# Mask rows of two batches copied by SyncE's transfers instead of VectorE, in a fused block-sparse attention and MLP kernel

## The chip, the cores and the metric

The kernel runs on one core of a Trainium2 chip. A core has five engines with queues of their own, each working in order: TensorE (PE, matmuls, with weight loads shown apart as PEld), VectorE (DVE), ScalarE (ACT), GpSimd (POOL), and SyncE (SP), which here does nothing but issue DMA transfers. They share an on-chip memory of 128 partitions (SBUF) and an accumulator memory for matmul results (PSUM); the inputs and outputs lie in the chip's main memory and move by DMA. The metric is the time of one execution in device microseconds.

## The reference

```python
# batch, n_heads, seq, head_dim = 4, 8, 768, 64
k_rep = k.reshape(B, H, 12, 64, D).mean(axis=3)            # one mean key per block of 64
gate = einsum('bhsd,bhnd->bhsn', q, k_rep)                 # causal blocks only, else -1e9
top_idx = argsort(gate, axis=-1)[..., -3:]                 # the 3 best blocks of each query
mask = blocks in top_idx or the query's own block, and key position <= query position
attn = softmax(where(mask, 0.125 * q @ k.T, -1e9))
x = (attn @ v), heads side by side: 3072 tokens x 512
h = x @ w_in                                               # 512 x 2048
g = 0.5 * h * (1 + tanh(sqrt(2 / pi) * (h + 0.044715 * h**3)))
out = g @ w_out                                            # 2048 x 512
```

Inputs and output are float32; the kernel computes its matmuls in float16, except for the gate.

## The kernel before

The work is cut by batch and, in it, by pair of heads: pairs 0 to 15, four to a batch (`p`, with `HP = 4`). Every pair goes through `pre(p)`, then `heads2(p)` (batch 0) or `heads(p)` (batches 1 to 3). When the four pairs of a batch are done, `s1(b)` computes the first layer of the MLP and its GELU, and the second layer follows: `s2_plain` for batch 0, and `s2` for the others, where the product is done with seven half-size products instead of eight (sums on DVE: `w_sums` for the weights, `sums` for the activations). The last batch does a part of the first layer in that way too (`s1_seven`).

In `pre(p)` for a pair of batches 1 to 3, four transfers of SyncE bring each of keys and queries in a layout that one DVE transpose (L564) turns into 128 rows (two heads of 64 dimensions) by 768 positions, in float32. From the keys DVE takes the block sums (L621); two copies with a cast to float16, one per head (`kc_all`, drawn by the helper `copy`, whose lines are L363 for ACT, L365 for POOL and L367 for DVE), bring them to `kT16[i][h]`, rows 0 to 63. The queries go the same way into `qT16[i][h]`. PE multiplies queries and block sums (the gate, L687), DVE transposes the result (L703), finds the third largest of 12 for each query with ten `max` instructions (L719), and writes a small table `madd` of 0 and -1 (L724).

The mask reaches the scores as 12 more rows: rows 64 to 75 of `qT16[i][h]` hold the mask of a query for 12 blocks, and the same rows of `kT16[i][h]` hold a constant pattern (`fill`, L520), so that a score matmul of 76 rows (L1046) adds the mask by itself. For these rows `madd` has to be transposed. For batch 1 (`byPE`) PE does it (L756) into a PSUM bank. For batches 2 and 3 a transposing DMA of SyncE (`mask_dma`, L763) writes a tile `mT`, of which there are two. Then `mc(h)` copies the 12 rows of one head and 640 positions into `qT16[i][h]`, two copies per pair; from `mT` DVE does them. The score matmuls of a head wait for the cast key, the cast query and this copy.

In `heads(p)` the scores of a unit go to a wide PSUM tile (L1046), ACT takes the exponential (L1059), POOL clears what lies above the diagonal (L1073), and PE multiplies by the values (L1085). DVE normalizes (L968, L969). The first layer is L1122, its GELU L1134; the second layer of batch 0 is L1322, the seven products are L1372 with their joins on DVE at L1421. Loads are L394 and L400, output rows L1347 and L1456, transposing DMAs of the normalized output L993. The weights are loaded by POOL's queue (L460); a small transfer on SyncE (L1567) waits for w_in to have landed, and the loads of batch 1 stand behind it.

The order is fixed in the file. Each step is an `Op` with its possible engines and a planning cost for each. `ORDER` lists the numbers of the steps in the order in which they are emitted, `BUFFER` says which buffer each takes, and `ENGINE` which steps run on another engine than their first; each engine executes its own steps in the order of that list. The list may also hold dummy matmuls (`warm`, L1524) which multiply zeros into a free bank; 72 are defined, and those that the list names are run. Here 39 are.

Of the kernel before, what the change touches and what calls it, by code (L numbers as in the profile page):

```python
# [189 lines left out]
    "POOL": [  # L190
        586, 587, 646, 647, 707, 972, 973, 1035, 1036, 1097, 1098,
        1159, 1160, 1425, 1489, 1551, 1612]}


class Op:
# [40 lines left out]
def kernel(  # L236
# [9 lines left out]
    nc = tc.nc  # L246
# [111 lines left out]
    add = plan.add  # L358
# [1268 lines left out]
```

## Time and profile before

| | us |
|---|---|
| median of 3 runs | 257.65 |
| lowest, highest | 257.62, 258.15 |
| the profiled execution | 257.76 |
| span in its profile, first to last instruction | 256.04 |
| granted TensorE clock | 1.0 of full |

| engine | busy, us | share | instructions |
|---|---|---|---|
| PE | 246.5 | 96% | 2485 |
| DVE | 191.4 | 75% | 539 |
| ACT | 176.4 | 69% | 225 |
| POOL | 84.3 | 33% | 163 |

A row of the profile names the line, the engine, the operation, `out<-in` by the program's names, sizes and a count; `L1046 PE ... wide<-qT,kT` writes a wide PSUM tile from `qT` and `kT`. In the groups, busy time in all and the mean in ns of one follow, then the idle time of the engine just ahead of these instructions and what ended it. In rows in order of time the first two numbers are start and length in us; in square brackets stands how long the engine was idle before and what released it. A tile's view gives minimum, median and maximum in ns. In a table of stages, each engine's busy time stands with its instruction count. The chain of waits is the chain of work that ended last, followed back from the last instruction. A busy PE is not PE at its peak: matmuls are pipelined, so the distance of starts, not the length of one, says how much PE time a matmul takes.

### The profile page before, as it was taken

The numbers are of one execution on the slowest core, as the hardware profiler recorded it, in microseconds if no ns is written. First come the engines' busy times: TensorE is split into PE (matmuls) and PEld (weight loads), VectorE is DVE, ScalarE is ACT, GpSimd is POOL, SyncE is SP. The second block draws the span as 40 slices with busy tenths as digits, with TensorE's granted clock in tenths as the row PEclk, the third lists the DMA queues.
The fourth block names the chain that finished last, engine by engine and source line by source line (L and its number), as shares of the span: only waits on it lengthen the run. The fifth ranks groups of instructions, "written<-read, shape, count | busy, mean of one in ns | idle before, by whom it ended". The sixth has DMA issues, their size and how long they took to land.

```text
span 256.0 us, 6451 instructions
## 1 busy us (share of the span) xinstructions
PE 246.5 (96%) x2485; PEld 171.2 (67%) x2485; DVE 191.4 (75%) x539; ACT 176.4 (69%) x225; POOL 84.3 (33%) x163
## 2 busy tenths in 40 slices
PE   7889999999998999999899999999999999999994
PEld 5667686555554566555578888555777786766883
DVE  2769751041989889989999999699889665579954
ACT  2399997634898998667969884566889957557300
POOL 8465970000239366223053853100056620000000
PEclk9999999999999999999999999999999999999999
DMA  8997599999989995999899699532112520040024
GB/s 164 218 208 166 94 212 191 213 161 157 184 142 165 153 143 99 172 179 199 127 174 110 144 188 166 118 94 69 26 34 72 64 74 1 3 165 0 3 82 164
DMA packets 130927, 32.62 MB, mean 127 GB/s; under 512 B 124528, under 2 KB 126928, under 8 KB 130896
## 3 DMA queue, kind: packets, MB, share of 16 engines
q1 hardware_dynamic: 126160, 27.62, 65.4%
q0 software_dynamic: 3136, 4.19, 9.7%
q10 hardware_dynamic: 1600, 0.39, 0.8%
q8 instruction: 19, 0.31, 0.5%
q14 instruction: 12, 0.10, 0.1%
HBM read 27.26 MB, written 6.29 MB: 131 GB/s over the span
## 4 chain that ended last, share of the span: by engine, by line
PE 51%; DVE 16%; SPq 11%; DMA 10%; POOL 4%; issue 3%; ACT 3%; ACTq 1%; DVEq 0%; POOLq 0%
PE bank L1372 17%; PE wide L1122 10%; SPq L400 9%; PE wide L1046 6%; PE wide L1211 5%; DMA w_in<-in_moe_w_in_dram 5%; PE bank L1085 5%; PE bank L1322 3%; DVE qT L367 3%; DMA sd<-in_k_dram 3%; DVE sel L719 2%; DVE s L564 2%; DVE XS L1309 2%; DMA G<-in_q_dram 2%; ACT ats L882 1%
## 5 line engine op out<-in xcount | busy, mean ns | idle before, releaser
L1122 PE MATMUL wide<-xT,w_in 128*128 128x384 f16 x416 | 72.6, 326 | 0.0
L1059 ACT ACTIVATE ats<-wide 128x896 f16<-128x896 f32 x72 | 63.4, 915 | 8.9 <-PE wide L1046 6.2
L1134 ACT ACTIVATE G<-wide 128x768 f16<-128x768 f32 x52 | 42.1, 810 | 27.3 <-PE wide L1122 27.0
L1122 PEld LDWEIGHTS <-w_in 128*128 128x128 f16 x416 | 40.0, 98 | 26.8 <-issue 1.3
L1073 POOL TENSOR_SCALAR_AFFINE_SELECT ats<-ats 128x256 f16<-128x256 f16 x72 | 33.3, 475 | 60.3 <-ACT ats L1059 60.2
L1046 PE MATMUL wide<-qT,kT 76*128 76x512 f16 (+3 forms) x192 | 39.1, 305 | 0.1
L564 DVE STREAM_TRANSPOSE s<-sd 128x768 f32<-128x768 f32 x24 | 23.1, 968 | 18.7 <-DMA sd<-in_k_dram 17.2
L1372 PE MATMUL bank<-w_out,G 128*128 128x256 f16 x216 | 31.4, 272 | 0.0
L1372 PEld LDWEIGHTS <-G 128*128 128x128 f16 x288 | 26.9, 98 | 6.0 <-issue 0.3
L1322 PE MATMUL bank<-w_out,G 128*128 128x512 f16 x96 | 28.1, 379 | 0.0
L365 POOL CAST kT<-s 64x768 f16<-64x768 f32 x17 | 15.2, 891 | 37.5 <-DVE s L564 37.0
L1421 DVE TENSOR_TENSOR osb<-bank,osb 128x512 f32<-128x512 f32 (+1 forms) x38 | 22.1, 592 | 5.1 <-PE bank L1372 4.5
L1085 PEld LDWEIGHTS <-ats 128*128 128x128 f16 x504 | 22.2, 98 | 3.9 <-POOL ats L1073 0.4
L1085 PE MATMUL bank<-v,ats 128*128 128x65 f16 x504 | 24.4, 194 | 0.2 <-POOL ats L1073 0.2
L1046 PEld LDWEIGHTS <-kT 76*128 76x128 f16 x192 | 17.3, 98 | 10.5 <-issue 0.8
L1372 PEld LDWEIGHTS <-XS 128*128 128x128 f16 x216 | 20.0, 98 | 5.5 <-DVE XS L1309 1.5
L1372 PE MATMUL bank<-TS,XS 128*128 128x256 f16 x144 | 22.0, 272 | 0.8 <-DVE XS L1309 0.7
L882 ACT ACTIVATE ats<-wide 128x1024 f16<-128x1024 f32 (+3 forms) x24 | 20.8, 924 | 1.3 <-PE wide L863 0.8
L365 POOL CAST v<-vsd 128x768 f16<-128x768 f32 x13 | 11.4, 875 | 13.8 <-DMA vsd<-in_v_dram 8.8
L969 DVE TENSOR_TENSOR xn<-bank,zr 128x384 f16<-128x384 f32 x24 | 13.4, 558 | 0.8
L719 DVE MAX8 sel<-sel 128x8 f32<-128x12 f32 x160 | 13.2, 158 | 0.6
L1322 PEld LDWEIGHTS <-G 128*128 128x128 f16 x96 | 8.9, 98 | 6.1 <-issue 0.3
(120 smaller groups left out, 358.6 us busy)
## 6 DMA issues: line engine op xcount, KB each, us to landing
out_dram<-osb SPq DMA_DIRECT2D x23, 256.0 KB
vsd<-in_v_dram SPq DMA_DIRECT2D x26, 192.0 KB
sd<-in_k_dram SPq DMA_DIRECT2D x48, 96.0 KB
sd<-in_q_dram SPq DMA_DIRECT2D x48, 96.0 KB
w_in<-in_moe_w_in_dram POOLq DMA_DIRECT2D x2, 1024.0 KB, 11.5
w_out<-in_moe_w_out_dram POOLq DMA_DIRECT2D x2, 1024.0 KB, 14.5
G<-in_k_dram SPq DMA_DIRECT2D x4, 192.0 KB
G<-in_q_dram SPq DMA_DIRECT2D x4, 192.0 KB
```

The lines of the kernel that those rows point to most:

```text
L365: nc.gpsimd.tensor_copy(out=out, in_=in_)
L400: nc.sync.dma_start(out=T[key, p][64 * hh + 32 * a:64 * hh + 32 * a + 32], in_=SRC[key][b, 2 * hp + hh].rearrange("(t i) (a j) -> a i t j" ...
L564: nc.vector.transpose(out=T[key + "T32", p], in_=T[key, p].rearrange("p t j -> p (t j)"))
L882: nc.scalar.activation(out=T["at", u][:, :, 0:n], in_=plan.buf[("st",) + u].rearrange("p (h w) -> p h w", h=2)[:, :, 0:n], func=AF.Exp, bi ...
L1046: nc.tensor.matmul(st[:, x:e], kT16[i][h][0:76, s0:s0 + 128], qT16[i][h][0:76, s0 + (x - cb):s0 + (e - cb)], start=True, stop=True)
L1059: nc.scalar.activation(out=T["at", u][:, 0:n], in_=plan.buf[("st",) + u][:, 0:n], func=AF.Exp, bias=0.0, scale=SCALE)
L1073: nc.gpsimd.affine_select(out=dg, in_=dg, compare_op=ALU.is_ge, fill=0.0, base=0, pattern=[[0, 2], [1, 128]], channel_multiplier=-1)
L1085: nc.tensor.matmul(pvv[:, qc, 0:65], at[:, cb + (qc - jc) * 128: cb + (qc - jc + 1) * 128], v16[i][:, jc, h, :], start=(gi == 0 and jc == ...
L1122: nc.tensor.matmul(hps[:, 512 * e:512 * e + HALF], w_in16[:, ci, (2 * j + e) * 128: (2 * j + e + 1) * 128], T["xT", b][:, ci, HALF * h:HAL ...
L1134: nc.scalar.activation(out=G[:, :, h, j, :], in_=plan.buf["hps", b, j, h].rearrange("p (e w) -> p e w", e=2)[:, :, 0:HALF], func=AF.Gelu_a ...
L1322: nc.tensor.matmul(plan.buf["ops", b, ti], G[:, f % 2, 2 * ti // NC, f // 2, ti % (NC // 2) * 128:ti % (NC // 2) * 128 + 128], w_out16[:, ...
L1372: nc.tensor.matmul(dst[:, HD * h:HD * h + HD], FACT[m][0][:, j, t * 128:(t + 1) * 128], FACT[m][1][:, j, :], start=(clear and j == 0), sto ...
```

## The change

Three edits to the steps, and a new `ORDER`, `BUFFER` and `ENGINE` for them.

1. For pairs 8 to 15 the two mask copies of DVE become one step of SyncE with two transfers, of 12 partitions and 640 float16 values each, from `mT` into `qT16[i][h]`. Both heads' scores now depend on that one step, which is planned at 1.2 on SyncE and 2.2 until it has landed.
2. The casts of the keys may also run on ACT, at 0.84.
3. The order is new throughout: every queue's instructions stand in another sequence, other steps go to other engines, and the list names 28 dummy matmuls.

```diff
-            kcs = [add({DVE: 0.56, POOL: 0.85}, kc_all(h),
+            kcs = [add({DVE: 0.56, POOL: 0.85, ACT: 0.84}, kc_all(h),
                        [t, old.get("k", None)], pr + 0.1) for h in range(2)]
...
-            mcs = [add({DVE: 0.5, ACT: 0.7} if byPE else {DVE: 0.33}, mc(h),
-                       [m, old.get("s")], pr) for h in range(2)]
-            add({"NONE": 0.0}, lambda _: None, mcs, pr,
+            def mc_dma(_):
+                for h in range(2):
+                    nc.sync.dma_start(
+                        out=qT16[i][h][64:76, 128:S],
+                        in_=T["mT", p][64 * h:64 * h + 12, :])
+            mcs = ([add({DVE: 0.5, ACT: 0.7}, mc(h), [m, old.get("s")], pr)
+                    for h in range(2)] if byPE else
+                   [add({SP: 1.2}, mc_dma, [m, old.get("s")], pr,
+                        lag=2.2)] * 2)
+            add({"NONE": 0.0}, lambda _: None, mcs if byPE else mcs[:1], pr,
                 gives=[("mk", p, 0) if byPE else ("mT", p)])
```

In the built program this gives, by engine: DVE loses 16 mask copies and 7 key casts and gets one cast of a query, one mask copy from a PSUM bank, and a few bank copies more or less; ACT gets 10 key casts and gives up one query cast; POOL has 14 key casts instead of 17; SyncE issues 16 transfers more; PE has the same matmuls apart from the dummies.

More of the change, by code (lines that the diff above doesn't have):

```diff
@@ L21 @@
 ORDER = [
[134 rows of a table removed]
-BUFFER = [
[24 rows of a table removed]
[132 rows of a table added]
+BUFFER = [
[24 rows of a table added]
 ENGINE = {
     "ACT": [
[5 rows of a table removed]
[6 rows of a table added]
     "POOL": [
-        586, 587, 646, 647, 707, 972, 973, 1035, 1036, 1097, 1098,
-        1159, 1160, 1425, 1489, 1551, 1612]}
+        337, 338, 587, 646, 647, 708, 973, 1034, 1156, 1421, 1484,
+        1544, 1605, 1606]}
 class Op:
```

325 rows, old and new, of tables (BUFFER, ENGINE, ORDER) are left out of this document.

## The prediction

> **What bounds the kernel now.** I read the page first (span, busy times, the shares of the chain), then the busy times by stage, then PE's order of time around its waits, then DVE's and SyncE's around the same moments, then the groups of the instructions that the change touches.
>
> ```profile
> span 256.0 us, 6451 instructions
> PE 246.5 (96%) x2485; PEld 171.2 (67%) x2485; DVE 191.4 (75%) x539; ACT 176.4 (69%) x225; POOL 84.3 (33%) x163
> PE 51%; DVE 16%; SPq 11%; DMA 10%; POOL 4%; issue 3%; ACT 3%; ACTq 1%; DVEq 0%; POOLq 0%
> ```
> ```profile
> 41.60:81.74 40.14, 38.95 (x282) 21.88 (x281) 20.67 (x62) 27.41 (x35) 8.47 (x15) 1.00 1.15 172
> 81.74:123.96 42.22, 42.18 (x396) 25.47 (x397) 38.64 (x111) 33.48 (x43) 17.13 (x28) 1.00 1.07 160
> 123.96:155.91 31.95, 31.02 (x366) 24.87 (x364) 31.14 (x71) 26.89 (x34) 17.11 (x31) 1.00 1.02 149
> 155.91:181.50 25.59, 25.59 (x211) 16.22 (x209) 22.26 (x84) 14.85 (x19) 0.88 (x2) 1.00 0.54 95
> 181.50:206.60 25.10, 24.86 (x317) 19.72 (x315) 19.21 (x40) 22.92 (x28) 14.09 (x27) 1.00 0.30 53
> ```
>
> In the stage table the columns are the stage, its length, and busy time of PE, PE's weight loads, DVE, ACT and POOL. PE is the bound: it idles 1.19 us from 41.60 to 81.74, 0.04, 0.93 from 123.96 to 155.91, 0.00, and 0.24 from 181.50 to 206.60. DVE is second: 38.64 of 42.22 and 31.14 of 31.95 in the two stages after 81.74. So DVE time freed is worth at most those short PE waits, which are here:
>
> ```profile
> 80.17 0.38 PE L1085 MATMUL bank<-v,ats 128*128 128x65 f16 x7
> 81.74 0.45 PE L756 MATMUL bank<-ident,madd 128*128 128x128 f16 x5 [1.20 <-DVE madd L724]
> ...
> 123.96 0.55 PE L1046 MATMUL wide<-qT,kT 76*128 76x512 f16 x3
> ...
> 126.71 1.08 PE L1372 MATMUL bank<-TS,XS 128*128 128x256 f16 x6 [0.72 <-DVE XS L1309]
> ```
>
> The first wait is for the mask of pair 6 (pairs are numbered 0 to 15, four to a batch); the row at 123.96 is the first score of pair 8, the first user of the changed mask copies.
>
> **The change, part by part.** It names three things, and the new order adds a fourth, idle fillers. Their rows:
>
> ```profile
> L367 DVE COPY qT<-mT x16: 317/319/939, 120.0 to 193.1; 12x640 f16<-12x640 f16 x16
> L520 SPq DMA_DIRECT2D kT<-G x8: 713/714/934, 21.5 to 27.1; - x8
> L763 SPq DMA_TRANSPOSE mT<-madd x8: 1200/1238/2685, 106.6 to 182.8; - x8
> ```
> ```profile
> L367 DVE COPY qT<-mT 12x640 f16<-12x640 f16 x16 | 7.1, 445 | 0.4
> L367 DVE CAST kT<-s 64x768 f16<-64x768 f32 x7 | 4.1, 587 | 0.1
> L365 POOL CAST kT<-s 64x768 f16<-64x768 f32 x17 | 15.2, 891 | 37.5 <-DVE s L564 37.0
> L363 ACT CAST qT<-s 64x768 f16<-64x768 f32 x11 | 9.1, 827 | 0.2
> L1524 PE MATMUL bank<-XS 128*128 128x256 f16 x39 | 8.0, 329 | 1.1 <-DVE bmask L292 1.1
> ```
>
> *DVE.* The 16 mask copies go (7.1 us) and so do the 7 key casts (4.1). One cast of a query, one mask copy and a few bank copies come to DVE instead; it ends about 10 us lighter.
>
> *ACT and POOL.* The built order has 10 key casts on ACT (none before), 14 on POOL (17), none on DVE, and one query cast less on ACT. ACT gains 10 - 1 = 9 casts of 827 ns, 7.4 us; POOL loses 3 x 891 ns, 2.7 us. The cover for ACT's casts is its idle time: 42.22 - 33.48 = 8.7 us in the stage from 81.74 and 31.95 - 26.89 = 5.1 in the next. Cost nothing; if that cover were gone, each cast standing before an exponential that PE needs would cost up to 0.83.
>
> *Fillers.* Apart from the dummy matmuls of L1524, PE's instructions are the same; the order holds 28 of those instead of 39. Four of the lost ones stood at 230 us, seven between 33 and 70. A 256-column matmul in an unbroken run takes 16.39/150 = 0.109 us:
>
> ```profile
> 236.29 16.39 PE bank L1372 x150
> ```
>
> So PE has 11 x 0.109 = 1.20 us less to do.
>
> *Order.* Ahead of pair 6's mask transposes the new order puts 7 more second-layer matmuls (L1322) and a few scores, in my count 1.65 us, and 7 fillers less (0.76): PE arrives there 0.89 later. What it waits for there comes from the weights and keys, by DMA and DVE:
>
> ```profile
> 26.97 1.66 POOL L460 DMA_DIRECT2D w_in<-in_moe_w_in_dram  x2
> ```
> ```profile
> 27.89 13.66 DMA w_in<-in_moe_w_in_dram
> ...
> 65.65 3.15 DMA sd<-in_k_dram
> 68.80 0.81 DVE s L564
> 69.61 3.31 DMA sd<-in_k_dram
> ```
>
> The same number of exponentials and copies of ACT, and the same POOL work, stand ahead of the w_in transfer in both orders; the loads behind it stand in the same order up to pair 6; DVE's work from that pair's keys to its mask is the same but for one cast against one normalization. So I leave 81.74 where it is. Of the 1.20 of idle time ahead of it 0.89 is then filled with work that used to stand behind, and behind 81.74 PE has 1.20 + 0.89 = 2.09 us less to do. That is the gain if nothing else waits.
>
> *What gives it back: SyncE.* Between pair 6's mask and the first score of pair 8 PE now has 0.55 us less work (10 more L1372, 7 L1322 and some scores fewer), so it gets there at 123.4. The mask of pair 8 must by then have gone through SyncE's queue, in order. How fast that queue issues:
>
> ```profile
> 98.96 0.52 SPq L394 DMA_DIRECT2D vsd<-in_v_dram  x1
> ...
> 106.57 2.69 SPq L763 DMA_TRANSPOSE mT<-madd  x1
> ...
> 113.08 1.80 SPq L400 DMA_DIRECT2D sd<-in_q_dram  x3
> ...
> 116.69 1.81 SPq L763 DMA_TRANSPOSE mT<-madd  x1
> ...
> 124.52 1.72 SPq L763 DMA_TRANSPOSE mT<-madd  x1
> ...
> 132.49 1.26 SPq L763 DMA_TRANSPOSE mT<-madd  x1
> ```
> ```profile
> 115.19 0.98 DVE L564 STREAM_TRANSPOSE s<-sd 128x768 f32<-128x768 f32 x1 [1.23 <-DMA sd<-in_q_dram]
> ```
>
> Twelve transfers are issued from 98.96 to 106.57: 0.634 each. The four transposes average 1.87. In the new order 18 transfers, pair 8's transpose, 4 loads, pair 9's transpose and 5 loads stand from that point to pair 8's two copies: 98.96 + 27 x 0.634 + 2 x 1.87 = 119.8; the copies are priced by the nearest row, the L520 transfers of 12 partitions, 2 x 0.714, so the second is issued by 121.2. Landing after the end of the issue: at least 115.19 - (113.08 + 1.80) = 0.31, at most the 3.31 that the chain waits for one load. I take 1.0, nearer the low end, since 15 KB follow a queue that lands its loads so soon there. Pair 8: 122.2, needed at 123.4, in time (121.5 to 124.5 by the bounds). Pair 9: 4 loads, a transpose, 2 loads and its copies later, 121.2 + 6 x 0.634 + 1.87 + 1.43 = 128.3, landing 129.3; PE's matmuls between the first scores of pairs 8 and 9, by their order and the spacing of their columns (0.109 for 256), are 6.1 us, needed at 129.5. Pair 10: 128.3 + 7 x 0.634 + 1.87 + 1.43 = 136.0, landing 137.0, needed 13.7 after pair 8, at 137.1. Pair 11: 136.0 + 11 x 0.634 + 1.43 = 144.4, landing 145.4, needed 20.6 after, at 144.0: 1.4 late. A single lateness moves PE once; the rest of the queue does not wait for PE. I take half of it, 0.7: the 0.634 per transfer has waits for buffers in it, which fall away where the queue is behind. Also queued behind the copies on SyncE are the loads of pairs 12 to 14 and the output rows; the loads come 8 x 0.714 = 5.7 us later at most and are used after 155, by a DVE that is then lighter. In batch 3 (16 - 8 = 8 copies) the queue is slack, DMA share 0.54 and 0.30: nothing.
>
> The Trainium skill, DMA: Bandwidth & Descriptors, "Anatomy of one DMA", speaks against the change: every DMA has about 2.0 us of fixed cost, mostly the receipt of the last byte, where a DVE copy here takes 0.32. By that figure, an estimate, each mask lands 1.0 us later than I take, and 1.7 would be given back instead of 0.7, a time of 257.4. No row of this trace shows the landing of a 12-partition copy.
>
> *Sum.* 1.20 (fillers) + 0.89 (idle time filled) - 0.7 (late masks) = 1.4 us. The profiled execution took 257.76 (256.04 of span and 1.72 around it), 0.11 above the median of 257.65. 257.76 - 1.4 = 256.4.
>
> **Rivals.**
> *More comes free.* DVE is lighter where PE waits for it at 126.7: from pair 6's mask to the last weight sum, four mask copies are gone. If masks are never late and the 0.93 and 0.24 us of idle PE also go, the gain is 2.09 + 1.17 = 3.3: 254.5. For it: DVE is 97% busy in that stage. Against: the queue's margins above are 1.2 us at most.
>
> *The gain is not on the path.* PE reaches the second layer's sums at 126 earlier, and waits there for DVE as before, since the XS sums stand behind as many other DVE instructions; only the four late fillers (0.44) remain: 257.3 to 257.8. For it: the 0.72 wait shows that DVE, not PE, sets that moment. Against: the two copies at 120 us, gone now, are on DVE directly ahead of it.
>
> *Slower: the masks queue behind SyncE's loads.* One mechanism at one place, pairs 8 to 11: with landings at the 3.31 bound, pair 8 comes 1.2 late, pair 9 2.2, pair 10 2.3, pair 11 3.8. It decides from a lateness of 2.6 us upwards (2.09 is used up, and 0.5 more): at 3.8, 257.76 - 2.09 + 3.8 = 259.5; with the transposes at 2.69 instead of 1.87, four of them, 3.3 more, near 262. For it: SyncE issues without a gap in that stretch, and DMA share is 1.02 to 1.07. Against: the q loads at 113 landed 0.31 after their issue.
>
> **How the numbers follow.** Forecast 0.42, its own range 255.6 to 257.1; more free 0.15; not on the path 0.15; slower 0.28, most of it at 258.2 to 259.5. Faster by over 0.2% (0.5 us, about what a measurement of this kernel can tell from none) is the first two, 0.57; within it the third, 0.15; slower 0.28. 254.9 cuts half of the second case, 259.4 the upper part of the fourth.
>
> **What would show it.** Right: 16 SyncE transfers into qT of about 0.7 us and no DVE copy from mT; 28 fillers; PE's wait ahead of pair 6's mask about 0.3; PE idle before the first scores of pairs 8 to 11 (L1046 of kernel before) below 1 us in sum. Wrong: a w_in transfer issued much after 27 us, which moves 81.74; score matmuls of pairs 8 to 11 that wait for qT's transfers by more than 2.6 us; exponentials on ACT that wait behind key casts while PE waits for them.

## The result, and the profile after

The changed kernel is slower. Its median is 260.5 us against 257.7 for the kernel before, a ratio of 1.0103 (95% interval 1.0073 to 1.0133). One of its eight executions took 877.7 us at full clock; it is left out of the ratio, and why it was slow is not known. Run again later beside other kernels it took 259.79 against 257.94, 1.0082 (1.0051 to 1.0113). The prediction was 256.4, so 3.4 to 4.1 us are to be explained.

First the page of the changed kernel: span, busy times, shares of the chain.

```profile
span 259.3 us, 6426 instructions
PE 246.7 (95%) x2474; PEld 169.6 (65%) x2474; DVE 183.5 (71%) x520; ACT 180.9 (70%) x231; POOL 79.0 (30%) x160
PE 67%; DMA 11%; DVE 9%; SPq 6%; issue 3%; ACT 3%; POOL 1%; DVEq 0%; POOLq 0%; ACTq 0%
```

DVE is 7.9 us lighter, as intended (about 10 were forecast), and PE has 11 instructions fewer, yet PE idles 12.6 us where it idled 9.5. The stages, with the columns of the table of before:

```profile
41.60:81.74 40.14, 40.10 (x288) 22.00 (x286) 20.60 (x64) 27.58 (x36) 9.46 (x17) 1.00 1.05 165
81.74:123.96 42.22, 41.29 (x392) 24.84 (x391) 38.73 (x121) 35.49 (x46) 12.82 (x23) 1.00 1.05 167
123.96:155.91 31.95, 30.26 (x364) 24.13 (x362) 27.80 (x51) 28.34 (x35) 14.91 (x30) 1.00 0.95 163
155.91:181.50 25.59, 23.60 (x178) 13.97 (x177) 20.59 (x82) 12.65 (x17) 0.00 (x0) 0.93 0.59 113
```

The idle 1.19 us ahead of pair 6's mask are gone (0.04 now). But PE now idles 0.93, 1.69 and 1.99 us in the three stages that follow, where it idled 0.04, 0.93 and 0.00. PE's rows in order of time show where; the last number in brackets is the wait, and the name behind it is what ended it:

```profile
80.78 0.44 PE L755 MATMUL bank<-ident,madd 128*128 128x128 f16 x5
...
83.75 0.54 PE L1053 MATMUL wide<-qT,kT 76*128 76x512 f16 x3 [0.42 <-ACT ats L1066]
...
131.05 0.54 PE L1053 MATMUL wide<-qT,kT 76*128 76x512 f16 x3 [0.84 <-DMA qT<-mT]
...
142.10 0.39 PE L1092 MATMUL bank<-v,ats 128*128 128x65 f16 x7 [0.85 <-POOL ats L1080]
...
163.21 0.48 PE L686 MATMUL bank<-s,ksb 128*32 128x160 f32 x8 [1.38 <-DVE s L563]
164.14 0.49 PE L686 MATMUL bank<-s,ksb 128*32 128x160 f32 x4 [0.46 <-DVE ksb L637]
```

Only the wait at 131 is for a mask copy (pair 9). The largest, 1.84 us at 163, stands at the gates of pairs 14 and 15, a step that the prediction did not look at. Behind each of the three places stands SyncE's queue. These are DVE's, SyncE's and POOL's rows there:

```profile
162.18 1.84 DVE L563 STREAM_TRANSPOSE s<-sd 128x768 f32<-128x768 f32 x2 [2.95 <-DMA sd<-in_q_dram]
```
```profile
154.81 3.87 SPq L399 DMA_DIRECT2D sd<-in_q_dram  x6
```
```profile
157.85 4.20 DMA sd<-in_q_dram
```
```profile
140.86 0.83 POOL L364 CAST v<-vsd 128x768 f16<-128x768 f32 x1 [2.29 <-DMA vsd<-in_v_dram]
141.64 0.77 POOL L1080 TENSOR_SCALAR_AFFINE_SELECT ats<-ats 128x256 f16<-128x256 f16 x2
```

At 162 DVE waits 2.95 us for the last queries, which SyncE issued until 158.7; the chain shows the last of these loads from the start of its issue, 157.85, to its landing 4.20 us later. At 141 POOL, which works in order, waits 2.29 us for a v load, and the causal selects behind the cast come late.

One more thing is in this execution: the clock. The stage from 155.91 has 0.93 of the granted clock, and the drop begins right behind the wait at 163:

```profile
163.00:165.00 2.00, 1.34 (x17) 0.49 (x18) 1.96 (x5) 0.00 (x0) 0.00 (x0) 0.78 0.01 4
165.00:167.00 2.00, 2.00 (x7) 0.91 (x6) 1.90 (x15) 0.00 (x0) 0.00 (x0) 0.50 0.00 0
167.00:169.00 2.00, 2.00 (x12) 1.16 (x11) 1.86 (x15) 0.85 (x2) 0.00 (x0) 0.86 0.41 81
```

That costs this execution 0.07 x 25.59 = 1.8 us. Three of the seven executions compared had a mean clock of 0.993 (spans 259.3, 259.5, 260.2); three had 1.000 (257.3, 258.0, 258.4) and one 0.998 (258.2). When the kernel was run again, one of six had a low clock (0.987). So some executions pay for the clock; at full clock the span is 1.3 to 2.4 us above the 256.0 of before.

### The profile page after: what moved, and what is told of

The parts are those of the page before. It is cut to its first block, busy times and chain, and to the rows that moved or that the text cites. A ratio compares the mean times of both kernels' runs of the same rounds, so it can differ in the third digit from the quotient of the medians.

```text
span 259.3 us, 6426 instructions
## 1 busy us (share of the span) xinstructions
PE 246.7 (95%) x2474; PEld 169.6 (65%) x2474; DVE 183.5 (71%) x520; ACT 180.9 (70%) x231; POOL 79.0 (30%) x160
## 4 chain that ended last, share of the span: by engine, by line
PE 67%; DMA 11%; DVE 9%; SPq 6%; issue 3%; ACT 3%; POOL 1%; DVEq 0%; POOLq 0%; ACTq 0%
PE bank L1379 19%; PE wide L1129 19%; PE wide L1053 7%; PE wide L1218 5%; SPq L399 4%; PE bank L1329 4%; PE bank L1092 3%; DMA sd<-in_q_dram 3%; PE wide L870 3%; DMA vsd<-in_v_dram 2%; PE bank L938 2%; DMA sd<-in_k_dram 2%; ACT ats L1066 2%; DVE s L563 2%; DMA G<-in_k_dram 2%
## 5 line engine op out<-in xcount | busy, mean ns | idle before, releaser
L1129 PE MATMUL wide<-xT,w_in 128*128 128x384 f16 x416 | 74.7, 330 | 0.0
L1066 ACT ACTIVATE ats<-wide 128x896 f16<-128x896 f32 x72 | 62.7, 915 | 7.2 <-PE wide L1053 6.0
L1080 POOL TENSOR_SCALAR_AFFINE_SELECT ats<-ats 128x256 f16<-128x256 f16 x72 | 31.2, 447 | 75.1 <-ACT ats L1066 42.3
L364 POOL CAST kT<-s 64x768 f16<-64x768 f32 x14 | 11.8, 842 | 24.9 <-DVE s L563 24.4
## 6 DMA issues: line engine op xcount, KB each, us to landing
out_dram<-osb SPq DMA_DIRECT2D x23, 256.0 KB
```

Source lines behind the costliest of these rows:

```text
L364: nc.gpsimd.tensor_copy(out=out, in_=in_)
L1066: nc.scalar.activation(out=T["at", u][:, 0:n], in_=plan.buf[("st",) + u][:, 0:n], func=AF.Exp, bias=0.0, scale=SCALE)
L1080: nc.gpsimd.affine_select(out=dg, in_=dg, compare_op=ALU.is_ge, fill=0.0, base=0, pattern=[[0, 2], [1, 128]], channel_multiplier=-1)
L1129: nc.tensor.matmul(hps[:, 512 * e:512 * e + HALF], w_in16[:, ci, (2 * j + e) * 128: (2 * j + e + 1) * 128], T["xT", b][:, ci, HALF * h:HAL ...
```

## The experiments

In each diff the lists are shown where they change; steps that move keep their buffers. Theory 1: the new order asks for something before SyncE delivers it. Theory 2: the mask copies hold SyncE's queue, and everything behind them is late. Times are medians, the kernel before beside them from the same chip.

**Late gates.** The gates of pairs 14 and 15 (steps 1549, 1610) stand later in PE's order.

```diff
-1488, 1549, 1428, 1489, 1490, 953, 1610, 1598
+1488, 1428, 1489, 1490, 953, 1598
...
-1242, 1493, ... 1229, 1236
+1242, 1549, 1493, ... 1229, 1610, 1236
```

> The changed kernel with one edit: the gate matmuls of pairs 14 and 15 (L686) stand 2.0 and 3.9 us of matmuls later in PE's order, behind 6 and 12 first-layer matmuls of batch 2 that wait for nothing. Theory 1, the new order asks for these gates before their queries are there: the waits of 1.38 and 0.46 us at 163 go, the clock has no idle PE to drop after, and the time falls from 260.5 by 1.8 to 2.6 us, to 257.9 to 258.7. Theory 2, SyncE's queue is late as a whole: the wait comes back at the next user (masks of pairs 14 and 15, first scores), and the time stays above 259.8.

Measured: 257.92 against 257.76, ratio 1.0001 (0.998 to 1.0022). Both waits at the gates are gone, and nothing took their place there; what is left are the mask and POOL:

```profile
131.38 0.54 PE L1053 MATMUL wide<-qT,kT 76*128 76x512 f16 x3 [0.71 <-DMA qT<-mT]
143.13 0.39 PE L1092 MATMUL bank<-v,ats 128*128 128x65 f16 x7 [1.40 <-POOL ats L1080]
```

Moving two steps of 0.5 us takes away 0.8% (1.0082 to 1.0001), 2.1 us, for a wait of 1.84, and the two intervals do not meet: the largest part of the loss was the place of these gates. The granted clock of the profiled execution was 0.993 again, this time lost around 19 to 22 us, behind a PE wait of 1.86 that ended at 17.36, so the wait at 163 is not the only place where the clock drops.

**Mask copies back on DVE**, in the new order.

```diff
-                    nc.sync.dma_start(
+                    nc.vector.tensor_copy(
                         out=qT16[i][h][64:76, 128:S],
                         in_=T["mT", p][64 * h:64 * h + 12, :])
```

The step of pair 8 moves ahead of 1161, those of pairs 12 and 13 ahead of 1248, so that DVE does not stand waiting for the transpose.

> The changed kernel with the 16 mask copies back on DVE, each pair's two about as far ahead of its first score as in the kernel before, order and casts otherwise as changed. It frees 16 x 0.73 = 11.7 us of SyncE's queue, 5.8 of it ahead of the last loads of batch 3. Theory 2 (the copies hold SyncE's queue and so the loads): the last query loads land 4 to 6 us earlier, the PE waits of 1.84 us at 163 and of 0.84 at 131 go, 257.3 to 258.5. Theory 1 (the order alone): PE waits at 157 to 164 remain within 0.5 us of 1.8 because DVE has the copies to do instead, 259.5 to 260.8.

Measured: 258.27 against 257.76, 1.0018 (1.0009 to 1.0028). The waits of PE, summed by what ended them (in all, times, longest):

```profile
PE wide L1053 <- DVE qT L366: 1.0, 2, 0.8
PE bank L686 <- DVE s L563: 0.6, 1, 0.6
PE bank L686 <- DVE ksb L637: 0.2, 1, 0.2
```

The 0.6 is at 120, for a gate of batch 2. The gates of pairs 14 and 15, at their early place, wait 0.18 us for the sums of keys and nothing for queries: with eight of the 16 copies, 5.8 us of issue, gone ahead of them, DVE takes the last queries up at 160.58 instead of 162.18, 1.6 us earlier (4 to 6 were expected), and that is enough. So both theories hold half of it: gates that early fail only with a queue that full, and the full queue hurts only gates that early. In exchange DVE, with pair 9's copies ahead of a query cast, is late with that cast (0.84).

**Mask copies on SyncE alone**, in the old order, at DVE's old places.

```diff
+                    if not byPE:
+                        nc.sync.dma_start(out=qT16[i][h][64:76, 128:S],
+                                          in_=src[64 * h:64 * h + 12, :])
+                        return
                     copy(eng, qT16[i][h][64:76, 128:S],
```

> The kernel before with the mask copies alone on SyncE, at the places in the order where DVE had them; casts, fillers and order as before. By the trace of before, SyncE is past the transpose of pair 9 at 118.5, of pair 10 at 126.2 and of pair 11 at 133.8, and the copies follow, so all are in time by 1 to 2 us with a landing of 2.0. Theory 1 (the fault is the new order's): 257.0 to 258.2. Theory 2 (the copies hold the loads of pairs 13 to 15 back by up to 5.8 us): the gates of pairs 14 and 15 at 167.8 wait, 258.7 to 261.

Measured: 257.70 against 257.76, 1.0001 (0.9989 to 1.0013). The edit that gives the change its name is worth nothing by itself, neither way. PE's 0.72 for DVE's sums at 126 is gone, but two other waits came:

```profile
131.04 0.39 PE L1089 MATMUL bank<-v,ats 128*128 128x65 f16 x7 [1.30 <-POOL ats L1077]
140.55 0.55 PE L1050 MATMUL wide<-qT,kT 76*128 76x512 f16 x3 [0.66 <-DMA qT<-mT]
```

**Late gates, and pair 9's mask copies early** (step 1046 directly behind 984 on SyncE).

```diff
-984, 1410, ... 1414, 1046, 1468
+984, 1046, 1410, ... 1414, 1468
```

> The changed kernel with the gates of pairs 14 and 15 late as in the run with that edit alone, and the mask copies of pair 9 issued on SyncE directly behind those of pair 8, ahead of the loads of pair 12's queries. Theory 1: beside the 1.8 us at 163 the wait of 0.84 us at 131 goes, 257.0 to 257.9, level with the kernel before or faster by up to 0.3%. Theory 2: 259 or more. If only the wait at 131 goes and comes back as a wait for POOL's exponentials near 142 (0.85 us there now), it equals the run with late gates alone.

Measured: 258.49 against 257.76, 1.0026 (1.0008 to 1.0045), not better than late gates alone. The mask's wait went, and the waits for POOL grew from 1.40 at 143 to, in all,

```profile
PE bank L1092 <- POOL ats L1080: 2.3, 2, 1.9
```

because pair 11's v load now stands behind these copies (POOL takes it up at 130.65, at 130.28 with late gates alone) and PE, without the wait for the mask, is there earlier: the longest, 1.89, is now at 133, and 0.46 is left at 142. So the last case of the expectation is what happened: the wait came back as one for POOL, though at another place.

**Key casts on ACT alone**, in the old order (586, 707, 972, 1036, 1097, 1098, 1160, 1426, 1488, 1551 in the list of ACT).

> The kernel before with one edit: the ten key casts that the changed kernel has on ACT (pairs 5, 7, 8, 9, 10 twice, 11, 12, 13, 14) run on ACT at their old places in the order; eight leave POOL, two leave DVE. The prediction's step (ACT's idle time covers them, cost nothing): 257.3 to 258.2. Rival: casts of 0.83 us stand ahead of exponentials that PE waits for, two to four of them on the path: 258.8 to 261.

Measured: 259.01 against 257.81, 1.0048 (1.0035 to 1.0060). The rival was right for the old order. The three longest of PE's new waits, all for ACT (a fourth is 0.45 at 143):

```profile
78.55 0.54 PE L1046 MATMUL wide<-qT,kT 76*128 76x512 f16 x2 [0.61 <-ACT ats L1059]
86.84 0.48 PE L687 MATMUL bank<-s,ksb 128*32 128x160 f32 x8 [0.68 <-ACT osb L363]
106.12 14.46 PE L1122 MATMUL wide<-xT,w_in 128*128 128x384 f16 x88 [0.94 <-ACT G L1134]
```

These four are 2.68 us in all; the waits of 1.20 at 81 and of 0.72 at 126 that the kernel before had are gone, and PE idles about 1.1 us more.

**Eleven fillers less**, in the old order (1917 to 1923 and 1925 to 1928 dropped).

> The kernel before without eleven of its fillers: seven of the eleven dummy matmuls between 33 and 70 us and the four at 230. The prediction's step (each filler is 0.109 us of PE's path): 1.20 less, 256.3 to 256.7. Rival: the seven stand ahead of PE's wait for pair 6's mask, which grows by their 0.76, and only the four late ones can count: 257.1 to 257.8.

Measured: 257.00 against 257.81, 0.9967 (0.9954 to 0.9979): 0.8 of the 1.20 expected. PE waits longer for pair 6's mask, 1.58 instead of 1.20, but at 126 it waits 0.36 for DVE's sums instead of 0.72, so these two cancel:

```profile
81.40 0.45 PE L756 MATMUL bank<-ident,madd 128*128 128x128 f16 x5 [1.58 <-DVE madd L724]
```

The 0.8 comes from the seven early fillers. Ahead of the four late ones PE is already 0.82 us earlier than in the kernel before (first row before, second row this run), and the span is 0.8 us shorter (255.2 instead of 256.0), so the four late ones gained nothing:

```profile
226.62 1.46 PE L1122 MATMUL wide<-xT,w_in 128*128 128x384 f16 x8
```
```profile
225.80 1.46 PE L1122 MATMUL wide<-xT,w_in 128*128 128x384 f16 x8
```

Where a late filler was left out, the matmuls on both sides of it start as far apart as before (0.33 us at 230, and within 0.02 us at the other three): it stood in a gap. The rival had it the wrong way round.

**Late gates, and v early**: the second halves of v of pairs 11 and 12 directly behind the first.

```diff
-1149, 1406, ... 1105, 1150, ... 1414, 1046, ... 1529, 1415, 1473
+1149, 1150, 1406, ... 1105, ... 1414, 1415, 1046, ... 1529, 1473
```

> The changed kernel with late gates (as in the run with that edit alone, 257.92), and the second halves of the v loads of pairs 11 and 12 issued on SyncE directly behind their first halves, which puts them ahead of the mask copies of pairs 9 and 10. Theory: POOL, in order, stands at its cast of v for that load (0.9 and 3.0 us with late gates alone), the causal selects behind it come late and PE waits 1.40 us for them at 143; with the halves early this wait goes: 256.3 to 257.2. Rival: SyncE's queue only passes the lateness on, to pair 9's mask or pair 12's keys, and PE's idle time stays: 257.6 to 258.6.

Measured: 257.67 against 257.81, 1.0002 (0.9986 to 1.0018), the same as late gates alone. POOL's 1.40 went; the wait for masks rose from 0.71 to

```profile
PE wide L1053 <- DMA qT<-mT: 1.4, 3, 0.8
```

**Late gates, v early, pair 9's mask early**, the last two edits together.

> As the run with late gates and early v halves, and pair 9's mask copies directly behind pair 8's. Theory: with v out of the way, the early mask copies no longer push v back as they did before (1.89 us at 133 for POOL's selects), and the 0.71 at 131 for the mask goes too: 0.5 to 0.8 less than the run without this edit, 255.7 to 256.6. Rival: what stands behind the copies (pair 12's queries, the transposes of pair 10's mask) is late instead, no gain: within 0.3 of that run, or slower.

Measured: 257.35 against 257.81, 0.9978 (0.9963 to 0.9994). Neither edit gained alone; together they may give 0.2%, though the interval overlaps with those of the runs with one edit less.

**Pair 14's queries early**, gates where the change has them: step 1534 directly behind 1533 on SyncE.

```diff
-1533, 1530, ... 1548, ... 1534
+1533, 1534, 1530, ... 1548
```

> The changed kernel, gates where they are, with one edit on SyncE: the last three query loads of pair 14 directly behind its first one, some 17 us earlier, instead of behind all of pair 15's. Theory 1, the gates stand too early for the loads as SyncE's order has them: the DVE transposes at 162.2 no longer wait 2.95 us, PE's 1.84 us at 163 shrink to under 0.6, 257.9 to 259.0. Rival, the loads are held by the length of the queue and not by their place: pair 15's queries land as late as pair 14's did, the wait stays at one gate, 259.6 to 260.8.

Measured: 259.59 against 257.94, 1.0076 (1.0057 to 1.0095). The wait at the gates shrank from 1.84 to 0.42 as theory 1 said, but the time did not follow (257.9 to 259.0 were expected): three loads issued earlier put pair 11's mask copies behind them, and PE waits 2.15 there.

```profile
148.93 0.54 PE L1053 MATMUL wide<-qT,kT 76*128 76x512 f16 x3 [2.15 <-DMA qT<-mT]
164.19 0.48 PE L686 MATMUL bank<-s,ksb 128*32 128x160 f32 x8 [0.42 <-DVE ksb L637]
```

**The changed kernel again**, unedited, beside the run above and the two below.

> The changed kernel itself once more, on the chip of the other runs of this call: 259.0 to 261.9 as before, if the difference to the runs with one edit is theirs and not the chip's.

Measured: 259.79 against 257.94. Its profiled execution has a clock of 1.00 throughout and a span of 258.2; PE idles 2.66 and 1.75 us in the stages from 123.96 and from 155.91:

```profile
123.96:155.91 31.95, 29.29 (x348) 23.31 (x346) 26.56 (x51) 27.36 (x35) 15.33 (x30) 1.00 0.98 157
155.91:181.50 25.59, 23.84 (x201) 14.77 (x199) 21.83 (x82) 14.02 (x18) 0.34 (x1) 1.00 0.61 119
```

**The changed kernel mended**: late gates; 984, 1046, 1150 in a row on SyncE (pair 8's and 9's mask copies, then v of pair 11); 1415 behind 1414; fillers 1907 to 1909 dropped.

> The changed kernel with late gates; pair 9's mask copies and the second half of pair 11's v directly behind pair 8's copies, so that neither mask nor v is pushed past its need; the second half of pair 12's v behind its first; and without the three fillers between 33 and 70 us. Theory (the three waits found are all that the new order lost): the 0.79 us wait of the run with early v and mask for pair 8's mask goes too, and up to 0.3 of fillers: 256.0 to 256.9. Rival (the queue passes lateness on, to pair 12's queries or the sums): 257.2 to 258.2.

Measured: 257.11 against 257.94, 0.9964 (0.9950 to 0.9978): by the medians 2.7 us less than the changed kernel unedited beside it, and 0.8 less than the kernel before. One wait is left in the two stages, 1.93 us for pair 10's mask at 140.

**Masks on SyncE and eleven fillers less**, in the old order.

> The kernel before with both edits that cost nothing there: mask copies on SyncE and eleven fillers less; order and casts as before. If the two add up: 0.0 and -0.8, 256.7 to 257.2. If the lighter DVE now counts, because with fewer fillers PE waits for it at 126 (0.36 us): 256.3 to 256.7. If PE, being earlier, meets late masks: 257.3 to 258.

Measured: 256.96 against 257.94, 0.9968 (0.9951 to 0.9985): the two simply add up, 0 and 0.8.

**The mended kernel with ACT's key casts back** on POOL and DVE.

> The mended changed kernel (257.11) with the ten key casts of ACT back on POOL (eight) and DVE (pairs 12 and 13), at their places in the order. If ACT's casts cost in the new order as they did in the old one (1.2 us): 255.6 to 256.4. If the new order covers them (PE's waits for ACT there are 0.43, 0.3 and 0.3 us): 256.8 to 257.5. If POOL, in order, then delays its selects by the casts: 257.6 to 259.

Measured: 256.67 against 257.63, 0.9976 (0.9958 to 0.9994), where the mended kernel had 0.9964. In the new order ACT's casts cost nothing that can be told.

**The mended kernel, pair 10's mask copies earlier** (1107 ahead of 1472).

> The mended changed kernel with pair 10's mask copies ahead of the first query load of pair 13, the transposes of pair 11's mask, an output row and a v load on SyncE, some 3 us earlier. If the lateness can be removed: PE's wait of 1.93 us at 140 goes, 255.2 to 256.0. If the queue passes it on (pair 11's mask and copies come 1.6 us later): a wait for pair 11 or for the gates takes its place, 256.5 to 257.8.

Measured: 259.03 against 257.63, 1.0054 (1.0040 to 1.0067). Pair 10's wait of 1.93 went, and its neighbour took it:

```profile
147.00 0.54 PE L1053 MATMUL wide<-qT,kT 76*128 76x512 f16 x3 [1.62 <-DMA qT<-mT]
```

The median is worse than that exchange explains. Part of it is the clock: three of the five executions had 0.993 (258.57, 259.03, 259.24), the profiled one, the fastest at 257.94, had 1.00. One at 1.00 took 259.32 all the same; what it lost was not found.

**All fifteen fillers after 33 us dropped**, in the old order.

> The kernel before without all fifteen fillers that stand after 33 us (the run with eleven gone took 257.00, 0.81 less than before). If the late four (0.44) and half of the others were the gain: another 0.2 less, 256.6 to 256.9. If PE's wait for pair 6's mask takes all four: 256.9 to 257.1. If fillers keep the clock up and fifteen fewer lower it: above 257.3 and a granted clock below 1 after 33 us.

Measured: 256.79 against 257.63, 0.9961 (0.9948 to 0.9973), a gain of 0.84, about that of eleven; the time lies in the first range of the expectation, but not by its reason, as the late four bring nothing. The clock of the profiled execution stayed at 1.00 in every stage from 41.60 to 236.30. By the ratios the fastest kernels are this one, the mended one and the two with eleven fillers less, within each other's intervals; the old order gets there without SyncE's copies and ACT's casts.

## Why the prediction was wrong, by its steps

*Fillers, -1.20.* Right for the work: in the execution of the changed kernel at full clock PE is busy 245.1 us instead of 246.5. As a gain it was too large in the old order, where 0.81 was measured: the seven early fillers paid in full (0.76 by the prediction's price), the four late ones (0.44) not at all, because they stood in gaps of PE. The rival "not on the path" had kept just those four.

*Idle time ahead of pair 6's mask, -0.89, with the mask staying at 81.74.* PE's transposes came at 80.78 without any wait, so this gained 1.15 us of idle time, more than said. So the mask did not stay at 81.74. But the stage directly behind gave back 0.89 (0.93 idle instead of 0.04), 0.42 of it at 83.75 for an exponential that ACT took up only after a mask copy of batch 1, as the chain shows:

```profile
82.07 0.69 ACT qT L362
82.78 0.93 ACT ats L1066
```

Work that fills a wait arrives at the next one earlier; the prediction counted the first and not the second.

*Late masks, +0.7.* The mechanism held; the place did not, and the size agrees by luck: it was half of a lateness of 1.4 at pair 11, and what was paid is a wait at pair 9, which was to be in time, of 0.84 us here and 1.11 when run again. The copies of pairs 8 to 11 were issued by 122.1, 129.6, 136.6 and 145.2, against the 121.2, 128.3, 136.0 and 144.4 worked out. The landing, taken as 1.0 after the end of the issue, was 1.33 for the one that PE waited for, which the chain shows from the start of its issue:

```profile
128.86 2.05 DMA qT<-mT
```

The Trainium skill's figure of about 2.0 us (DMA: Bandwidth & Descriptors, "Anatomy of one DMA") agrees with that 2.05, counted from the start of the issue; the section states it for transfers issued by GpSimd, and the prediction had counted it from the end, which gave its estimate 0.7 us too much. Each copy holds SyncE for 0.73 us, near the 0.71 that the prediction took:

```profile
L805 SPq DMA_DIRECT2D qT<-mT x16: 716/728/849, 120.5 to 183.1; - x16
```

*ACT's casts, nothing.* ACT is 4.5 us heavier (7.4 were forecast). Right in the new order (casts back: no difference), wrong as an argument: idle time in a stage is no cover for an engine that works in order. In the old order, where ACT has 183.5 us of work with them against 180.9 here, the same ten casts cost 1.2 us.

*Batch 3, "the loads come 5.7 us later at most and are used after 155, by a DVE that is then lighter": nothing.* This is the step that failed. It compared the loads with the use that the kernel before made of them. The bound on their lateness held: by the run with the copies back on DVE it is 1.6 us. But in the kernel before the last query load was issued at 161.9, even later than now (157.85), and PE did not wait (0.00 idle in that stage), because the gates stood as two and two, 7 us apart:

```profile
160.62 0.75 PE L687 MATMUL bank<-s,ksb 128*32 128x160 f32 x16
...
167.80 0.75 PE L687 MATMUL bank<-s,ksb 128*32 128x160 f32 x16
```

In the new order all four gates stand between 156.8 and 164.1. That was to be seen in the order itself, which lists these steps, before any run. A "lighter DVE" does not help a DVE that waits for data. Cost: 1.84 us of idle PE, 2.1 us of time by the run with late gates, and in some executions the clock behind it.

*Not in the prediction at all: v loads.* The mask copies also stand ahead of v loads, POOL waits for those in order with its selects behind, and PE waits 0.85 to 1.4 us at 142. The rival "slower" named SyncE's queue as the culprit, but only masks behind loads; the larger loss was loads behind masks.

So the sum in the end, by the execution of the changed kernel at full clock (span 258.2 against 256.0): PE has 1.35 us less to do and idles 3.5 us more. Of the idle time 1.16 is gained ahead of pair 6's mask; 0.62 is lost directly behind it, 1.73 from 123.96 to 155.91 (waits of 1.11 for pair 9's mask and of 1.32 and 0.23 for POOL), 1.75 at the gates, and some 0.5 in small pieces elsewhere. In some executions up to 1.8 more goes by the clock. Inside the full queue lateness was mostly only moved: four edits that brought one transfer forward turned its wait into one for another (0.71 for a mask into 0.9 more at POOL, 1.40 at POOL into 0.7 more for masks, 1.84 at the gates into 0.42 there and 2.15 for a mask, 1.93 for a mask into 1.62 for the next). What helped was moving the *need*, two gates that PE could do later at no cost.

## What to carry to other kernels

When work moves to a queue that already issues without a gap, add up what the queue must deliver and by when for every user behind it, not only for the moved work: here the masks were nearly in time, and the queries and values behind them were not. When a change brings a new order, list the first users of each late load in both orders; a step that is moved forward by some microseconds may be the whole loss, and moving it back is cheaper than moving transfers. Idle time of an in-order engine in a stage says nothing on whether the next item of its list can wait. And work that is taken out pays only where the engine does not stand in a gap there anyway: here seven fillers paid and four did not.

## What the runs showed of the hardware that was not expected

A causal select on POOL, 0.41 us as a rule, took 2.96 in the old order with the masks on SyncE, and that is the wait of 1.30 us at 131 shown above. These are the selects of that run and of the kernel before (shortest, median, longest in ns), and DVE's rows at that time:

```profile
L1077 POOL TENSOR_SCALAR_AFFINE_SELECT ats<-ats x72: 397/406/2963, 70.6 to 207.1; 128x256 f16<-128x256 f16 x72
```
```profile
L1073 POOL TENSOR_SCALAR_AFFINE_SELECT ats<-ats x72: 397/406/1125, 70.6 to 206.4; 128x256 f16<-128x256 f16 x72
```
```profile
127.22 3.77 POOL L1077 TENSOR_SCALAR_AFFINE_SELECT ats<-ats 128x256 f16<-128x256 f16 x2 [5.56 <-ACT ats L1063]
```
```profile
128.03 1.02 DVE L1313 TENSOR_TENSOR XS<-G,XS 128x768 f16<-128x768 f16 x2
128.96 0.69 DVE L1295 TENSOR_TENSOR TS<-w_out,TS 128x1024 f16<-128x1024 f16 x1
129.56 0.56 DVE L1313 TENSOR_TENSOR G<-G 128x768 f16<-128x768 f16 x1
130.03 0.69 DVE L1295 TENSOR_TENSOR TS<-w_out,TS 128x1024 f16<-128x1024 f16 x1
130.63 0.69 DVE L1425 TENSOR_TENSOR osb<-bank,osb 128x512 f32<-128x512 f32 x1
```

The select ends at 130.99, 0.36 us after DVE has left its unbroken run of float16 additions with both operands in SBUF for a join that reads PSUM. The run with masks on SyncE and fewer fillers shows the same 2.96. The Trainium skill (SBUF — State Buffer, "SBUF: two separate sides") says that DVE and GpSimd share one pair of ports as a lock for a whole instruction, taken by DVE operations with two SBUF inputs among others; the rows fit. If it is this lock, it was not passed to POOL between five such instructions. In the kernel before, two mask copies stand between these additions. So freeing DVE may have made POOL slower at one place, and that may be why that edit gained nothing; no run took this alone away, and the cause is not shown.

The granted clock fell to 0.50 for some 3.4 us (the three rows from 163 to 169 in the section on the result lose 0.44, 1.00 and 0.28 us, 1.72 in all, half of 3.4) behind waits of 1.38 and 0.46 us in one profiled execution, and not in the other, which had waits of 1.28 and 0.45 there. With late gates it fell in the same way behind a wait of 1.86 us; in the profiled executions with a wait of 1.93 us (the mended kernel) and of 2.15 us (pair 14's queries early) it did not. The Trainium skill (TensorE: Matmul & The Clock Gate, "Part 1: The HAM clock gate") ties the clock to busy windows of about 3.4 us; the length of the drop agrees. What decides whether a wait of this length costs the clock, no run here shows. Fifteen fillers fewer in the old order did not bring it about.
